# An FFT-mixing and gated-FFN kernel: fp32 first pass, filter scaling on VectorE in program order, and a second pass in two batch halves

## The chip, the cores and the metric

The kernel runs on one core of one Trainium2 chip. The metric is the device time of one execution in microseconds (us). A core has five engines with queues of their own: TensorE (PE in the profile) for matmuls, VectorE (DVE) and ScalarE (ACT) for elementwise work, GpSimd (POOL), and SyncE (SP), which here only starts transfers. Each engine takes its instructions in order. Transfers run on 16 DMA engines beside them. Matmuls write to PSUM, the other operands lie in SBUF, and inputs, outputs and large intermediates lie in HBM.

## The reference, cut to what matters

```python
# x: (8, 3008, 256) fp32, filt_r, filt_i: (1505, 256) fp32
X = np.fft.rfft(x, axis=1)                       # along the sequence
Y = X * (filt_r + 1j * filt_i)[None]
y = np.fft.irfft(Y, n=3008, axis=1)              # (8, 3008, 256)
t = y.reshape(24064, 256)
gate = np.maximum(t @ w_gate, 0)                 # w_gate, w_val: (256, 1536)
out  = (gate * (t @ w_val)) @ w_out              # w_out: (1536, 256)
```

## The kernel before

The length 3008 is split as 64 x 47, so that the transform becomes small matrix products. There are four stages:

- Tables: sine and cosine matrices are computed on the chip. GpSimd writes index grids, VectorE multiplies them and reduces them to one period, ScalarE takes the sine. The filters are loaded and scaled, and the weights of the FFN are loaded and cast to bf16.
- Pass A: a transform over 64 points (`W1blk`), from `x` to the HBM buffer `Abuf`.
- Pass B: for each of 33 frequencies `k1` a transform over 47 points (`F2m`), the product with the filter, and the inverse over 47 points (`I2t`, `I2u`), from `Abuf` to the HBM buffer `Dbuf`.
- Pass C: for each of 8 x 6 blocks of up to 512 tokens the inverse over 64 points (`M1`) and then the FFN, from `Dbuf` to the output.

All pools are given to a scheduler that places the instructions of each engine by its own estimate, so the order on an engine is not that of the source. The parts that matter, cut:

```python
# ---- tables: one grid is built for F2 (2 halves of k1) and for I2 (2 halves) ----
def center(dst, src, ncols, modulus): ...   # six VectorE operations on 128 x ncols
def build_vgrid(stage, ks, kn): ...         # two iotas, then 4 + 2 * 6 VectorE operations -> grs, grc
def put(mats, rofs, cofs, src, ks, kn, sgn): # ScalarE: sine of grs or grc into F2m, I2t or I2u
    ...
# ---- filters: one staging buffer fstg for four blocks (r and i, two halves of k1) ----
fstg = genf.tile([128, KH, D], FP32, tag="fstg")
fmir2 = genf.tile([128, KH, D], BF16, tag="fmir2")
for (src_hbm, dst_tile, imag) in ((filt_r, Ftr, False), (filt_i, Fti, True)):
    for (ks, kn) in ((0, 17), (17, 16)):
        for rofs in (0, 64):
            nc.gpsimd.dma_start(fstg[rofs:rofs + 24, :kn, :], ...)
            nc.scalar.activation(dst_tile[rofs:rofs + 24, ks:ks + kn, :],
                                 fstg[rofs:rofs + 24, :kn, :], AF.Copy, scale=1.0 / 3008.0)
        for r in range(23):                       # mirrored rows, one transfer each
            nc.gpsimd.dma_start(fstg[32 + r:33 + r, :kn, :], ...)
        nc.scalar.activation(fmir2[32:55, :kn, :], rev[32:55], AF.Copy, scale=sgn / 3008.0)
        for rofs in (0, 64):
            nc.gpsimd.dma_start(dst_tile[rofs + 24:rofs + 47, ks:ks + kn, :], fmir2[32:55, :kn, :])
# ---- FFN weights: GpSimd loads to stgw (one buffer per shape), ScalarE casts ----
...
# ---- pass A: 4 pairs of batches x 6 tiles ----
for q in range(B // 2):
    for c0 in range(0, N2, 8):
        asb = pa.tile([128, 8 * D], BF16, tag="asb", bufs=3)
        xf = pa.tile([128, 8 * D], FP32, tag="xf", bufs=2)
        ldeng.dma_start(xf[:, :cnt * D], ...)                  # 1 MB; SyncE and ScalarE by turns
        xb = pa.tile([128, 8 * D], BF16, tag="xb", bufs=2)
        nc.vector.tensor_copy(xb[:, :cnt * D], xf[:, :cnt * D])
        for cc0 in range(0, cnt, 2):
            ps = psA.tile([128, 2 * D], FP32, tag="psa", bufs=2)
            nc.tensor.matmul(ps[:, :w], W1blk, xb[:, cc0 * D:cc0 * D + w], start=True, stop=True)
            nc.scalar.copy(asb[:, cc0 * D:cc0 * D + w], ps[:, :w])
        for bl in range(2):                                    # two stores to Abuf
            steng.dma_start(Abuf[:, c0:c0 + cnt, 2 * q + bl, :], ...)
# ---- pass B: 33 frequencies, all 8 batches (2048 columns) in two parts c ----
for k1 in range(NK1):
    at = atiles[k1 % 4]                                        # [128, B * D]
    nc.sync.dma_start(at[0:48, :], Abuf[k1])                   # and a second half for 1 <= k1 <= 31
    for c in range(2):
        psX = psB.tile([128, 1024], FP32, tag="psx")           # 2 buffers
        ...                                                    # 2 matmuls F2m x at
        nc.vector.tensor_tensor(tt, psX3, _bcast_mid(Ftr[:, k1, :], 4), op=ALU.mult)
        nc.vector.tensor_tensor(uu, psX3, _bcast_mid(Fti[:, k1, :], 4), op=ALU.mult)
        psD = psB.tile([128, 1024], FP32, tag="psd")           # 2 buffers
        ...                                                    # 4 matmuls I2t x tt + I2u x uu
        nc.scalar.copy(dsb[:, cs], psD)
    steng.dma_start(Dbuf[k1], dsb[0:48, :])                    # and a second for 1 <= k1 <= 31
# ---- pass C: 48 blocks ----
for b in range(B):
    for (z0, nb) in n2_blocks:
        dblk = pcd.tile([64, 8, D], BF16, tag="dblk")          # 4 buffers
        nc.sync.dma_start(dblk[:, :nb, :], Dbuf[:, z0:z0 + nb, b, :])
        ...        # psY = M1 x dblk, yt; 12 x (psG, psV, vsb, prod); 4 x (psO over 12, osb, store)
```

Of the kernel before, what the change touches and what calls it, by code (L numbers as in the profile page):

```python
# [9 lines left out]
FP32 = mybir.dt.float32  # L10
BF16 = mybir.dt.bfloat16
I32 = mybir.dt.int32
AF = mybir.ActivationFunctionType
ALU = mybir.AluOpType
# [15 lines left out]
def kernel(  # L30
# [10 lines left out]
    nc = tc.nc  # L41
# [4 lines left out]
    NK1 = 33  # L46
    DFF = moe_w_gate.shape[1]
    NFT = DFF // 128
    assert S == N1 * N2 and D == 256 and DFF % 128 == 0

    consts = ctx.enter_context(tc.tile_pool(name="consts", bufs=1))
    dram = ctx.enter_context(tc.tile_pool(name="dram", bufs=1, space=bass.MemoryType.DRAM))

# [34 lines left out]
        nc.scalar.activation(out_ap, rem[sl], AF.Sin, bias=0.0,  # L88
                             scale=scale_sign * 2.0 * math.pi / modulus)

    W1blk = consts.tile([128, 128], BF16)
    nc.vector.memset(W1blk, 0.0)
    for blk in range(2):
        rs = blk * 64
# [29 lines left out]
    with tc.tile_pool(name="passA", bufs=4) as pa, \  # L124
# [80 lines left out]
        for (src_hbm, dst_tile, imag) in ((filt_r, Ftr, False), (filt_i, Fti, True)):  # L205
            for (ks, kn) in ((0, 17), (17, 16)):
                for rofs in (0, 64):
                    nc.gpsimd.dma_start(fstg[rofs:rofs + 24, :kn, :],
                                        _ap(src_hbm, ks * D, [[64 * D, 24], [D, kn], [1, D]]))
                    nc.scalar.activation(dst_tile[rofs:rofs + 24, ks:ks + kn, :],  # L210
                                         fstg[rofs:rofs + 24, :kn, :],
                                         AF.Copy, bias=0.0, scale=1.0 / 3008.0)
                for r in range(23):
                    k2 = 24 + r
                    first_row = 3008 - 64 * k2 - (ks + kn - 1)
                    nc.gpsimd.dma_start(fstg[32 + r:33 + r, :kn, :],
                                        _ap(src_hbm, first_row * D, [[1, 1], [D, kn], [1, D]]))
                rev = dataclasses.replace(
                    fstg, offset=fstg.offset + (kn - 1) * D,
                    ap=[list(fstg.ap[0]), [-D, kn], [1, D]])  # L220
                sgn = -1.0 if imag else 1.0
                nc.scalar.activation(fmir2[32:55, :kn, :], rev[32:55], AF.Copy,
                                     bias=0.0, scale=sgn / 3008.0)
                for rofs in (0, 64):
                    nc.gpsimd.dma_start(dst_tile[rofs + 24:rofs + 47, ks:ks + kn, :],
                                        fmir2[32:55, :kn, :])
# [8 lines left out]
                                              [[fdim_hbm, 128], [128 * fdim_hbm, kdim], [1, fstep]]))  # L235
                nc.scalar.copy(w_sb[:, :, ci * fstep:(ci + 1) * fstep], stgw)

        with tc.tile_pool(name="psA", bufs=1, space=bass.MemoryType.PSUM) as psA:
            for q in range(B // 2):
                for c0 in range(0, N2, 8):  # L240
                    cnt = min(8, N2 - c0)
                    asb = pa.tile([128, 8 * D], BF16, tag="asb", bufs=3)
                    xf = pa.tile([128, 8 * D], FP32, tag="xf", bufs=2)
                    ldeng = nc.sync if (c0 // 8) % 2 == 0 else nc.scalar
                    ldeng.dma_start(xf[:, :cnt * D],
                                    x_rs[q * 128:(q + 1) * 128, c0:c0 + cnt, :])
                    xb = pa.tile([128, 8 * D], BF16, tag="xb", bufs=2)
                    nc.vector.tensor_copy(xb[:, :cnt * D], xf[:, :cnt * D])  # L248
                    for cc0 in range(0, cnt, 2):
                        ccnt = min(2, cnt - cc0)  # L250
                        w = ccnt * D
                        ps = psA.tile([128, 2 * D], FP32, tag="psa", bufs=2)
                        nc.tensor.matmul(ps[:, :w], W1blk, xb[:, cc0 * D:cc0 * D + w],  # L253
                                         start=True, stop=True)
                        nc.scalar.copy(asb[:, cc0 * D:cc0 * D + w], ps[:, :w])  # L255
                    for bl in range(2):
# [3 lines left out]
                            Abuf[:, c0:c0 + cnt, b, :],  # L260
                            asb[bl * 64:(bl + 1) * 64, :cnt * D].rearrange("p (a d) -> p a d", d=D))


    with tc.tile_pool(name="passB", bufs=4) as pb, \
         tc.tile_pool(name="psB", bufs=2, space=bass.MemoryType.PSUM) as psB:
        na_bufs = 4
        atiles = []
        for i in range(na_bufs):
            t = pb.tile([128, B * D], BF16, tag="ak1", name=f"ak1_{i}", bufs=na_bufs)
            nc.vector.memset(t, 0.0)  # L270
            atiles.append(t)
        for k1 in range(NK1):
            at = atiles[k1 % na_bufs]
            dsb = pb.tile([128, B * D], BF16, tag="dsb", bufs=3)
            nc.sync.dma_start(at[0:48, :].rearrange("p (b d) -> p b d", d=D),
                              Abuf[k1, :, :, :])
            if 1 <= k1 <= 31:
                nc.sync.dma_start(at[64:112, :].rearrange("p (b d) -> p b d", d=D),
                                  Abuf[32 + k1, :, :, :])
            for c in range(2):  # L280
                cs = slice(c * 1024, (c + 1) * 1024)
                psX = psB.tile([128, 1024], FP32, tag="psx")
                for h in range(2):
                    hs = slice(c * 1024 + h * 512, c * 1024 + (h + 1) * 512)
                    nc.tensor.matmul(psX[:, h * 512:(h + 1) * 512], F2m[:, k1, :],  # L285
                                     at[:, hs], start=True, stop=True)
                tt = pb.tile([128, 4, D], BF16, tag="t", bufs=3)
                uu = pb.tile([128, 4, D], BF16, tag="u", bufs=3)
                psX3 = psX.rearrange("p (a d) -> p a d", d=D)
                nc.vector.tensor_tensor(tt, psX3, _bcast_mid(Ftr[:, k1, :], 4), op=ALU.mult)  # L290
                nc.vector.tensor_tensor(uu, psX3, _bcast_mid(Fti[:, k1, :], 4), op=ALU.mult)  # L291
                psD = psB.tile([128, 1024], FP32, tag="psd")
                for h in range(2):
                    os_ = slice(h * 512, (h + 1) * 512)
                    nc.tensor.matmul(psD[:, os_], I2t[:, k1, :],  # L295
                                     tt.rearrange("p a d -> p (a d)")[:, os_],
                                     start=True, stop=False)
                    nc.tensor.matmul(psD[:, os_], I2u[:, k1, :],  # L298
                                     uu.rearrange("p a d -> p (a d)")[:, os_],
                                     start=False, stop=True)  # L300
                nc.scalar.copy(dsb[:, cs], psD)  # L301
            steng = nc.scalar if (k1 % 2 == 0) else nc.sync
            steng.dma_start(Dbuf[k1, :, :, :],
                            dsb[0:48, :].rearrange("p (b d) -> p b d", d=D))
            if 1 <= k1 <= 31:
                steng.dma_start(Dbuf[32 + k1, :, :, :],
                                dsb[64:112, :].rearrange("p (b d) -> p b d", d=D))

    out_rs = out.rearrange("(b n1 n2) d -> b n1 n2 d", n1=N1, n2=N2)
    n2_blocks = [(z, min(8, N2 - z)) for z in range(0, N2, 8)]  # L310

# [83 lines left out]
```

## Time and profile before

| what | value |
|---|---|
| median of 5 runs | 1274.94 us (1274.26 to 1279.07) |
| profiled execution | 1274.26 us, span of the trace 1272.5 us |
| busy, share of the span | PE 77%, VectorE 60%, ScalarE 41%, GpSimd 6% |
| granted TensorE clock, mean | 0.989 |
| pass A, pass B | 24 casts of x on VectorE, 96 matmuls; 66 products `tt` and 66 `uu` |
| DMA | 111.51 MB, 88 GB/s over the span |

The profile is a page with the busy time of each engine, a strip of 40 slices, the chain of work that ended last, and groups of equal instructions; the trace behind it answers questions about stretches of time, about single instructions in order of time, and about waits. A line of the order of time gives the start, the length, the engine, the line of the source (L followed by a number), the operation, what is written from what, and in square brackets the idle time before it and what ended it. `ACTq`, `SPq` and `POOLq` are the parts of these engines that start transfers. An engine that is busy for a large share of the whole span may still be idle in the stage that decides, so stages are looked at one by one.

### The profile page before, as it was taken

The page shows a single profiled execution, that of the slowest core. Times are in us where ns is not written, and L with a number is a line of the kernel's source. Part 1 is how long each engine was busy: PE and PEld are TensorE (multiplying, and loading weights), DVE is VectorE, ACT ScalarE, POOL GpSimd, SP SyncE. Part 2 cuts the span into 40 slices and gives each one's busy share as a digit, 9 for nine tenths or more (in the row PEclk, how much of TensorE's full clock was granted, in tenths as well). Part 3 has the DMA queues.
Part 4 walks back from the last instruction along what each step waited for, and adds up shares of the span by engine and source line. Part 5 has one row for each costly group of instructions (what it writes and reads, how often), then busy time and mean ns, then how long its engine had stood idle before and what let it go on. Part 6 is the DMA issues. An engine that isn't in the chain of part 4 may idle for free.

```text
span 1272.5 us, 16253 instructions
## 1 busy us (share of the span) xinstructions
PE 984.8 (77%) x5852; PEld 512.4 (40%) x5852; DVE 765.6 (60%) x1151; ACT 517.7 (41%) x787; POOL 70.3 (6%) x139
## 2 busy tenths in 40 slices
PE   0324420465565999999999999999999999999998
PEld 0000000121121545555555545555555555555555
DVE  7971220698696665566655665566655665566655
ACT  3564443645543343334333343334333343334433
POOL 2130016400100000000000000000000000000000
PEclk9999999999798999999999999999999999999999
DMA  3779973665753111111111111111111111111111
GB/s 103 225 208 281 314 162 80 146 198 164 211 167 97 29 46 51 47 39 38 48 49 51 34 39 51 50 36 37 51 48 46 35 45 48 50 34 42 39 34 32
DMA packets 96257, 111.51 MB, mean 88 GB/s; under 512 B 11960, under 2 KB 85624, under 8 KB 93240
## 3 DMA queue, kind: packets, MB, share of 16 engines
q1 hardware_dynamic: 75280, 74.88, 20.8%
q10 hardware_dynamic: 16192, 24.51, 6.1%
q0 software_dynamic: 4704, 11.08, 3.7%
q8 instruction: 46, 0.75, 0.3%
q14 instruction: 35, 0.29, 0.1%
HBM read 59.06 MB, written 49.81 MB: 86 GB/s over the span
## 4 chain that ended last, share of the span: by engine, by line
PE 63%; DVE 4%; issue 1%; DMA 0%; ACT 0%; DVEq 0%
PE psG L337 22%; PE psO L354 20%; PE psV L340 20%; DVE yt L330 2%; DVE osb L358 2%; PE psY L326 1%; DMA Dbuf<-dsb 0%; DVE prod L345 0%; DVE uu L291 0%; ACT dsb L301 0%; PE psD L298 0%; ACT vsb L343 0%; PE psD L295 0%; DVEq L330 0%
## 5 line engine op out<-in xcount | busy, mean ns | idle before, releaser
L343 ACT CAST vsb<-psV 128x512 bf16<-128x512 f32 (+1 forms) x576 | 323.0, 578 | 539.7 <-PE psV L340 523.3
L345 DVE SCALAR_TENSOR_TENSOR prod<-psG,vsb 128x512 bf16<-128x512 f32 (+1 forms) x576 | 380.9, 679 | 196.5 <-ACT vsb L343 171.2
L337 PE MATMUL psG<-yt,WgT 128*128 128x512 bf16 (+1 forms) x1152 | 345.3, 374 | 34.8 <-DVE yt L330 33.9
L340 PE MATMUL psV<-yt,WvT 128*128 128x512 bf16 (+1 forms) x1152 | 354.9, 376 | 0.1
L354 PE MATMUL psO<-WoT,prod 128*128 128x256 bf16 (+1 forms) x2304 | 281.6, 273 | 0.0
L354 PEld LDWEIGHTS <-prod 128*128 128x128 bf16 (+1 forms) x2304 | 221.7, 98 | 57.4 <-DVE prod L345 10.7
L358 DVE COPY osb<-psO 128x256 f32<-128x256 f32 x192 | 81.5, 425 | 145.6 <-PE psO L354 145.6
L340 PEld LDWEIGHTS <-WvT 128*128 128x128 bf16 x1152 | 107.9, 97 | 148.6 <-issue 34.7
L337 PEld LDWEIGHTS <-WgT 128*128 128x128 bf16 x1152 | 111.7, 97 | 138.1 <-issue 38.5
L253 PE MATMUL ps<-xb,W1blk 128*128 128x512 bf16 x96 | 51.0, 587 | 121.2 <-DVE xb L248 80.2
L298 PE MATMUL psD<-uu,I2u 128*128 128x512 bf16 x132 | 51.8, 396 | 98.6 <-DVE uu L291 98.6
L291 DVE TENSOR_TENSOR uu<-psX,Fti 128x1024 bf16<-128x1024 f32 x66 | 80.1, 1216 | 54.6 <-DMA Fti<-fmir 54.6
L301 ACT CAST dsb<-psD 128x1024 bf16<-128x1024 f32 x66 | 66.5, 1012 | 73.0 <-PE psD L298 68.3
L290 DVE TENSOR_TENSOR tt<-psX,Ftr 128x1024 bf16<-128x1024 f32 x66 | 80.2, 1217 | 12.7 <-PE psX L285 9.1
L253 PEld LDWEIGHTS <-W1blk 128*128 128x128 bf16 x96 | 9.7, 113 | 161.7 <-issue 71.3
L255 ACT CAST asb<-ps 128x512 bf16<-128x512 f32 x96 | 52.2, 579 | 50.7 <-PE ps L253 49.4
L295 PEld LDWEIGHTS <-I2t 128*128 128x128 bf16 x132 | 12.9, 98 | 147.7 <-issue 120.2
L248 DVE CAST xb<-xf 128x2048 bf16<-128x2048 f32 (+1 forms) x24 | 28.7, 1202 | 66.7 <-DMA xf<-in_x_dram 60.6
L330 DVE CAST yt<-psY 128x512 bf16<-128x512 f32 (+1 forms) x96 | 60.3, 669 | 9.1 <-PE psY L326 9.1
L295 PE MATMUL psD<-tt,I2t 128*128 128x512 bf16 x132 | 52.6, 398 | 10.3 <-ACT dsb L301 5.5
L326 PEld LDWEIGHTS <-dblk 64*128 64x128 bf16 x752 | 30.2, 95 | 57.0 <-issue 56.1
L326 PE MATMUL psY<-M,dblk 64*128 64x64 bf16 x752 | 46.5, 193 | 7.6 <-issue 7.6
(74 smaller groups left out, 288.2 us busy)
## 6 DMA issues: line engine op xcount, KB each, us to landing
out_dram<-osb SPq DMA_DIRECT2D x376, 64.0 KB, 2.0
xf<-in_x_dram SPq DMA_DIRECT2D x12, 1024.0 KB, 7.2
ak<-Abuf SPq DMA_DIRECT2D x64, 192.0 KB, 3.5
dblk<-Dbuf SPq DMA_DIRECT2D x40, 256.0 KB, 3.4
xf<-in_x_dram ACTq DMA_DIRECT2D x8, 1024.0 KB, 6.9
Dbuf<-dsb ACTq DMA_DIRECT2D x32, 192.0 KB, 3.6
Dbuf<-dsb SPq DMA_DIRECT2D x32, 192.0 KB, 3.2
Abuf<-asb SPq DMA_DIRECT2D x20, 256.0 KB, 4.6
```

The lines of the kernel that those rows point to most:

```text
L290: nc.vector.tensor_tensor(tt, psX3, _bcast_mid(Ftr[:, k1, :], 4), op=ALU.mult)
L291: nc.vector.tensor_tensor(uu, psX3, _bcast_mid(Fti[:, k1, :], 4), op=ALU.mult)
L295: nc.tensor.matmul(psD[:, os_], I2t[:, k1, :], tt.rearrange("p a d -> p (a d)")[:, os_], start=True, stop=False)
L301: nc.scalar.copy(dsb[:, cs], psD)
L326: nc.tensor.matmul(psY[:, j * 64:(j + 1) * 64], dblk[:, j, h * 128:(h + 1) * 128], M1, start=(j == 0), stop=(j == nb - 1))
L330: nc.vector.tensor_copy(yt[:, :ntok], psY[:, :ntok])
L337: nc.tensor.matmul(psG[:, :ntok], WgT[:, h, ft * 128:(ft + 1) * 128], yts[h][:, :ntok], start=(h == 0), stop=(h == 1))
L340: nc.tensor.matmul(psV[:, :ntok], WvT[:, h, ft * 128:(ft + 1) * 128], yts[h][:, :ntok], start=(h == 0), stop=(h == 1))
L343: nc.scalar.copy(vsb[:, :ntok], psV[:, :ntok])
L345: nc.vector.scalar_tensor_tensor(prod[:, :ntok], in0=psG[:, :ntok], scalar=0.0, in1=vsb[:, :ntok], op0=ALU.max, op1=ALU.mult)
L354: nc.tensor.matmul(psO[:tw, :D], prods[ft][:, t_i * 128:t_i * 128 + tw], WoT[:, ft, :], start=(ft == 0), stop=(ft == NFT - 1))
L358: nc.vector.tensor_copy(osb[:tw], psO[:tw, :D])
```

## The change

The change takes VectorE out of pass A and gives it the filters, and it lets pass C's first reads depend on half of pass B only:

1. `tc.manual_schedule` for VectorE: from the start to the end of pass B, VectorE runs its instructions in the order of the source, not in the scheduler's. The other engines are placed by the scheduler as before.
2. Pass A multiplies in fp32: `W1blk` is an fp32 table, the matmul reads `xf` directly, the cast to `xb` is gone, and `xf` has three buffers in place of two.
3. The filters are scaled on VectorE in place of ScalarE.
4. Pass B goes over the 33 frequencies twice, each time for four of the eight batches. The tiles `ak` and `dsb` and their transfers have half the size,[...] and the pools of pass A and pass B are open at the same time.

```diff
+    region = ctx.enter_context(ExitStack())
+    region.enter_context(tc.manual_schedule(engines={mybir.EngineType.DVE}))
...
-    W1blk = consts.tile([128, 128], BF16)
+    W1blk = consts.tile([128, 128], FP32)
...
-                    nc.scalar.activation(dst_tile[rofs:rofs + 24, ks:ks + kn, :],
-                                         fstg[rofs:rofs + 24, :kn, :],
-                                         AF.Copy, bias=0.0, scale=1.0 / 3008.0)
+                    nc.vector.tensor_scalar(dst_tile[rofs:rofs + 24, ks:ks + kn, :],
+                                            fstg[rofs:rofs + 24, :kn, :],
+                                            scalar1=1.0 / 3008.0, scalar2=None, op0=ALU.mult)
...
-                nc.scalar.activation(fmir2[32:55, :kn, :], rev[32:55], AF.Copy,
-                                     bias=0.0, scale=sgn / 3008.0)
+                nc.vector.tensor_scalar(fmir2[32:55, :kn, :], rev[32:55],
+                                        scalar1=sgn / 3008.0, scalar2=None, op0=ALU.mult)
...
-                    xf = pa.tile([128, 8 * D], FP32, tag="xf", bufs=2)
+                    xf = pa.tile([128, 8 * D], FP32, tag="xf", bufs=3)
...
-                    xb = pa.tile([128, 8 * D], BF16, tag="xb", bufs=2)
-                    nc.vector.tensor_copy(xb[:, :cnt * D], xf[:, :cnt * D])
...
-                        nc.tensor.matmul(ps[:, :w], W1blk, xb[:, cc0 * D:cc0 * D + w],
+                        nc.tensor.matmul(ps[:, :w], W1blk, xf[:, cc0 * D:cc0 * D + w],
                                          start=True, stop=True)
...
-        for k1 in range(NK1):                        # all 8 batches
-            at = atiles[k1 % na_bufs]                # [128, B * D], 4 buffers
+            def pass_b_half(half):
+                b0 = half * 4
+                for k1 in range(NK1):                # batches b0 .. b0 + 3
+                    at = atiles[ait % na_bufs]       # [128, 4 * D], 4 buffers
+                    nc.sync.dma_start(at[0:48, :], Abuf[k1, :, b0:b0 + 4, :])
...                                                   # psX of 1024 columns, tt and uu as before
+                    for c in range(2):
+                        psD = psB.tile([128, 512], FP32, tag="psd", bufs=2)
...                                                   # I2t x tt, I2u x uu
+                        nc.scalar.copy(dsb[:, cs], psD)
+                    steng.dma_start(Dbuf[k1, :, b0:b0 + 4, :], dsb[0:48, :])
...
+            for q in range(4):
+                pass_a_pair(q)
+            pass_b_half(0)
+            pass_b_half(1)
+
+    region.close()
```

(Cut: the rearrangements of the access patterns, the second transfers for `1 <= k1 <= 31`, and the unchanged lines.)

## The prediction

> **What bounds the kernel now.** I read first the chain that ended last, then the busy time by stage, then the order of time on ScalarE and VectorE around the stage borders.
>
> The chain on the page, by engine:
>
> ```profile
> PE 63%; DVE 4%; issue 1%; DMA 0%; ACT 0%; DVEq 0%
> ```
>
> It names only TensorE, and it runs almost entirely through the last stage, which the diff does not touch. So the question is when that stage starts. The busy time in five stretches (start:end, length, busy us per engine, clock, DMA share, GB/s):
>
> ```profile
> 0.00:87.00 87.00, 14.88 (x28) 3.07 (x29) 74.00 (x135) 41.96 (x56) 25.77 (x51) 1.00 0.57 174
> 87.00:173.00 86.00, 36.17 (x69) 6.67 (x67) 19.05 (x16) 40.93 (x74) 0.00 (x0) 1.00 0.86 271
> 188.00:236.00 48.00, 2.02 (x5) 0.69 (x5) 2.36 (x2) 22.82 (x7) 26.54 (x56) 1.00 0.39 86
> 236.00:402.00 166.00, 102.54 (x386) 33.30 (x384) 145.36 (x128) 81.58 (x74) 13.13 (x23) 0.95 0.60 174
> 407.00:1272.00 865.00, 826.00 (x5360) 467.64 (x5357) 518.81 (x864) 322.97 (x576) 0.00 (x0) 1.00 0.16 43
> ```
>
> Each stretch has its own limit: VectorE (74 of 87 us) while tables are built and pass A starts; DMA (86%) for the rest of pass A; nothing at all from 188 to 236; VectorE (145 of 166) in pass B; TensorE (826 of 865) in pass C. The hole from 188 to 236 shows in the order of time on ScalarE (start, length, instruction, wait before it):
>
> ```profile
> 172.88 0.61 ACTq L259 DMA_DIRECT2D Abuf<-asb  x1
> 173.82 3.83 ACT L222 ACTIVATE fmir<-fstg 23x4352 bf16<-23x4352 f32 x1 [0.97 <-ACT asb L255]
> ...
> 201.57 3.62 ACT L222 ACTIVATE fmir<-fstg 23x4096 bf16<-23x4096 f32 x1 [9.51 <-DMA fstg<-in_filt_i_dram]
> ...
> 223.42 3.83 ACT L222 ACTIVATE fmir<-fstg 23x4352 bf16<-23x4352 f32 x1 [6.73 <-DMA fstg<-in_filt_i_dram]
> ```
>
> The first filter block was loaded by about 89 us, but its scaling sits in ScalarE's queue behind the last pass-A copy. One buffer `fstg` serves four blocks, so the chain load, scale, reload starts at 174 and takes 22 to 27 us a block. VectorE pays for it:
>
> ```profile
> 232.71 2.36 DVE L291 TENSOR_TENSOR uu<-psX,Fti 128x1024 bf16<-128x1024 f32 x2 [45.69 <-DMA Fti<-fmir]
> ```
>
> At the border to pass C, TensorE waits for the last store and reload of Dbuf:
>
> ```profile
> 398.85 0.38 PE L298 MATMUL psD<-uu,I2u 128*128 128x512 bf16 x1
> ...
> 406.83 0.37 PE L326 MATMUL psY<-M,dblk 64*128 64x64 bf16 x4 [7.60 <-issue]
> ```
>
> [...] No run here shows an fp32 matmul yet; it is the largest unmeasured cost. [...] pass-A matmuls start 0.43 us apart, those of pass B 0.22 us, though the granted clock is 1.00 in both. [...] In the trace 12 filter loads took 7.32 us on GpSimd (0.61 each) beside busy VectorE and 0.48 beside an idle one: small.
>
> **The change part by part.**
>
> *1. Casts leave VectorE.* 24 casts of about 1.2 us (28.7 us in the groups) go; eight of them lie before 87 us. VectorE now runs in program order: small tables (about 52 dependent operations at 0.2 us and the start, near 13 us, and 2.5 of wait for M1f behind the first matmuls), three memsets of 1.82, then four grids. One grid without casts takes 11.2 us in the trace (75.8 to 87.0). So 15.5 + 5.5 + 4 x 11.4 + about 3 of waits = 70 us, against 87: minus 17. By then, as now at 87, about 8 of 24 x-tiles are through, because ScalarE's sine writes sit between the copies and wait for the grids.
>
> *2. fp32 matmuls in pass A.* [...] A tile has four: 4 us. The DMA now needs 5.1 us a tile (16 casts from 87.3 to 168.9), so TensorE fits under it[...]. The third xf buffer makes up for holding xf through the matmuls.
>
> *3. Filter scaling moves to VectorE.* 24x4352 took 3.83 us on ScalarE; the VectorE cast of 128x2048 took 1.22 us from SBUF, so about 2.4 us. Of more weight is its place: it comes after the grids and two memsets of 3.58 and so starts at 70 + 7 = 77 us, under pass A. First block done at about 84. A later block took 22 us (205.5 to 227.5); faster scaling takes off 1.5, but loads in a full DMA take longer: GpSimd waits for the load eight earlier, and 23 row loads at a latency of 5 instead of 3 us add about 5. So 26 a block: 84 + 3 x 26 = 162 us. Pass B's first product comes after that in VectorE's order.
>
> *4. Pass A ends.* Remaining work from 72 us is what took from 87 to 173 before: 86 us. In it now lie three filter blocks, at 31% of the DMA for 48 us over two blocks, or 7.5 us each: plus 22. Three buffers and an earlier start should raise the DMA share from 86% towards 95%: minus 10. 72 + 86 + 22 - 10 = 170. From the last copy to the first product took 12 us (172.8 to 184.7: store, load, matmul, and a little filter wait); I take 10. Pass B starts at 180, and the filter chain (162) is hidden with 18 to spare. Before, it ran from 232.7: 53 us gained.
>
> *5. Pass B in two halves of four batches.* As many products as before, of the same shape: 2 x 66, one each 1.133 us in steady state (239.86, 241.00, 242.13): 149.5 us. It took 165.7 (232.7 to 398.4); the late last filter block (8.9) and stalls for psX (9.1) made most of the rest. The filter waits go; the weight casts stay in ScalarE's queue ahead of some dsb copies, single-buffered: I leave 8 us. DMAs double in number at half the size: 4 in 2.27 us, landing in about 3.5; four `ak` buffers give 9 us of lead, enough. ScalarE copies two of 0.59 instead of one of 1.01 per 1024 columns: no bound. 180 + 149.5 + 8 = 337.5.
>
> *6. Border and pass C.* The first `dblk` tiles need only the first half of Dbuf, stored long before, so they are prefetched; the 7.6 us wait falls away and psY follows the last matmul, at about 339. Built, the changed program has pass C's instructions in the same order on every compute engine, but for the first two blocks on TensorE. Before, it took 1272.5 - 406.8 = 865.7. End 1204.5; the median before lies 2.4 above the profiled span: about 1206.
>
> Sum of the gains: 53 at the hole, 8 in pass B, 7.5 at the border: 68.5 us.
>
> **Rivals.**
> - *TensorE bounds pass A.* [...]2 us a matmul, 8 a tile, 16 tiles: pass A ends at 72 + 130 = 202, total near 1238. For it: no row shows such a matmul[...].
> - *The filter chain takes the place of pass A as the bound.* With latencies of 8 us, 34 us a block: 186, total near 1212. For it: the 86% DMA share. VectorE's strict order makes any lateness count in full.
> - *Pass A hides nothing:* what the filters took alone they take from the x loads; the plus 22 is that. If the share does not rise, 180 instead of 170: 1216.
> - *Stalls in pass B:* smaller DMAs and weight casts cost 20 instead of 8: 1218. If grids and DMA go better than thought, pass A ends at 155: 1190.
>
> **Range and chances.** Pass A's end carries plus or minus 12, pass B's stalls plus or minus 8, and the lean is upward[...]. Predicted 1206 us, 1188 to 1228 eight times in ten. Faster by over 2% means under 1249.4; even the worst rival stays below it, and only two rivals together would pass it: 0.93 faster, 0.05 within 2%, 0.02 slower.
>
> **What would show it.** The fp32 matmul's mean near 1 us and TensorE under 80% busy in pass A; `fmir` scaling on VectorE from about 82 us and its fourth at about 160; the first steady `tt` at 180, preceded by a wait for psX or the ak load and not for a filter; tt and uu back to back for 150 us; psY within 2 us of the last pass-B matmul; pass C 865 us long. A wait for `fstg` in front of the fourth `fmir` later than 175, or matmuls of 1.7 us and more, would prove steps 3 or 2 wrong.

## The result, and the profile after

| | before | after |
|---|---|---|
| median | 1276.47 us (16 runs, 1272.38 to 1280.44) | 1217.09 us (9 runs, 1213.77 to 1227.27) |
| ratio after / before | | 0.9547, 95% interval 0.9522 to 0.9573 |
| profiled span | 1272.5 us | 1214.8 us |
| pass C's first matmul | 406.83 us | 352.11 us |

The kernel is 4.5% faster. Pass C takes 862.7 us (1214.8 - 352.1) against 865.7, so nearly the whole gain is the time at which pass C starts. The chain that ended last, by engine, on the page of the changed kernel:

```profile
PE 66%; DVE 4%; issue 0%; ACT 0%; DVEq 0%
```

DMA has left the chain (the last Dbuf store and reload were in it before). The busy time in six stretches of the changed kernel (start:end, length, then busy us and count for PE, PE weight load, VectorE, ScalarE, GpSimd, then clock, DMA share, GB/s):

```profile
0.00:75.00 75.00, 40.68 (x67) 14.90 (x68) 63.66 (x125) 38.07 (x61) 24.93 (x50) 0.84 0.69 218
75.00:163.00 88.00, 67.19 (x126) 23.66 (x124) 30.66 (x11) 37.72 (x66) 35.19 (x55) 0.85 0.96 284
163.00:189.00 26.00, 0.00 (x0) 0.00 (x0) 9.25 (x5) 0.41 (x2) 17.61 (x29) 0.56 0.42 108
189.00:197.00 8.00, 1.01 (x2) 0.14 (x2) 1.99 (x5) 2.94 (x2) 2.66 (x4) 0.50 1.04 228
197.00:351.00 154.00, 118.14 (x394) 33.83 (x394) 149.36 (x132) 75.29 (x135) 1.55 (x3) 0.97 0.65 185
352.00:1214.00 862.00, 823.52 (x5360) 466.93 (x5359) 518.92 (x864) 323.06 (x577) 0.00 (x0) 1.00 0.16 43
```

The hole of 48 us (188 to 236 before) has not gone: it has shrunk to 34 us, from 163 to 197. In its first 26 us TensorE does nothing and the DMA is busy for 42%. What fills it is seen in VectorE's order of time (start, length, instruction, in brackets the wait before it and what ended it):

```profile
73.30 0.94 DVE L154 TENSOR_TENSOR grc<-grc,gq 128x752 f32<-128x752 f32 x1
...
87.81 4.68 DVE L224 TENSOR_SCALAR fmir<-fstg 23x4352 bf16<-23x4352 f32 x1
...
127.72 2.28 DVE L224 TENSOR_SCALAR fmir<-fstg 23x4096 bf16<-23x4096 f32 x1 [18.08 <-DMA fstg<-in_filt_r_dram]
...
160.54 4.67 DVE L224 TENSOR_SCALAR fmir<-fstg 23x4352 bf16<-23x4352 f32 x1 [13.92 <-DMA fstg<-in_filt_i_dram]
...
186.36 2.28 DVE L224 TENSOR_SCALAR fmir<-fstg 23x4096 bf16<-23x4096 f32 x1 [9.34 <-DMA fstg<-in_filt_i_dram]
188.81 2.11 DVE L270 MEMSET ak<- 128x512 uint32 x4 [0.17 <-issue]
196.76 1.22 DVE L294 TENSOR_TENSOR tt<-psX,Ftr 128x1024 bf16<-128x1024 f32 x1 [5.84 <-PE psX L289]
```

The four blocks of the filter end at 92.5, 130.0, 165.2 and 188.6: 37.5 and 35.2 us apart while pass A's transfers run, 23.4 once they are over. From the second on, each waits for a load into `fstg`. Pass B's first product stands behind the fourth. The memsets of `ak` stand there too, so the loads of `ak` cannot be asked for earlier; SyncE's waits (line, what it waited for, us in total, times, longest) have it, although the half of `Abuf` that is read had been complete for long (shown below):

```profile
SPq L281 <- DVE ak L270: 25.2, 1, 25.2
```

TensorE at both ends of pass B, in the order of time:

```profile
161.38 1.56 PE L256 MATMUL ps<-xf,W1blk 128*128 128x512 f32 x4 [0.23 <-ACT asb L258]
195.71 1.01 PE L289 MATMUL psX<-ak,F2m 128*128 128x512 bf16 x2 [32.77 <-DMA ak<-Abuf]
...
350.58 0.59 PE L302 MATMUL psD<-uu,I2u 128*128 128x512 bf16 x2 [0.35 <-DVE uu L295]
352.11 0.62 PE L336 MATMUL psY<-M,dblk 64*128 64x64 bf16 x16 [0.94 <-ACT dsb L305]
```

At the border to pass C the wait of 7.60 us is now 0.94. The fp32 matmuls have their own group on the page:

```profile
L256 PE MATMUL ps<-xf,W1blk 128*128 128x512 f32 x192 | 107.9, 712 | 55.1 <-ACT asb L258 38.5
```

There were 96 instructions and the group has 192 records: an fp32 matmul leaves two. In TensorE's order of time (the last line comes after a pause):

```profile
82.17 3.79 PE L256 MATMUL ps<-xf,W1blk 128*128 128x512 f32 x8 [0.23 <-ACT asb L258]
86.17 3.79 PE L256 MATMUL ps<-xf,W1blk 128*128 128x512 f32 x8 [0.22 <-ACT asb L258]
...
147.04 3.78 PE L256 MATMUL ps<-xf,W1blk 128*128 128x512 f32 x4 [4.09 <-ACT asb L258]
```

Eight records take 3.79 us in the first two lines, where most start 0.43 us apart and the granted clock is 1.00 (79 to 97 us). Four take 3.78 us in the last, where they start 0.85 us apart and the clock is 0.50 (147 to 151 us). The mean of 0.85 in pass A is made of such stretches.

### The profile page after: what moved, and what is told of

It reads as the page before. It is cut to its first block, busy times and chain, and to the rows that moved or that the text cites. A ratio compares the mean times of both kernels' runs of the same rounds, so it can differ in the third digit from the quotient of the medians.

```text
span 1214.8 us, 16712 instructions
## 1 busy us (share of the span) xinstructions
PE 1050.7 (86%) x5948; PEld 539.5 (44%) x5948; DVE 773.8 (64%) x1139; ACT 478.5 (39%) x841; POOL 81.9 (7%) x139
## 4 chain that ended last, share of the span: by engine, by line
PE 66%; DVE 4%; issue 0%; ACT 0%; DVEq 0%
PE psG L347 23%; PE psO L364 21%; PE psV L350 21%; DVE yt L340 2%; DVE osb L368 2%; PE psY L336 2%; DVE uu L295 0%; ACT dsb L305 0%; ACT vsb L353 0%; PE psD L302 0%; DVEq L340 0%
## 5 line engine op out<-in xcount | busy, mean ns | idle before, releaser
L256 PE MATMUL ps<-xf,W1blk 128*128 128x512 f32 x192 | 107.9, 712 | 55.1 <-ACT asb L258 38.5
L305 ACT CAST dsb<-psD 128x512 bf16<-128x512 f32 x132 | 71.1, 589 | 74.9 <-PE psD L302 73.4
L256 PEld LDWEIGHTS ps<-xf,W1blk 128*128 128x128 f32 x192 | 38.6, 225 | 124.0 <-ACT asb L258 93.7
L289 PE MATMUL psX<-ak,F2m 128*128 128x512 bf16 x132 | 40.9, 389 | 36.7 <-DMA ak<-Abuf 34.6
L302 PE MATMUL psD<-uu,I2u 128*128 128x512 bf16 x132 | 41.5, 388 | 19.0 <-DVE uu L295 15.4
L224 DVE TENSOR_SCALAR fmir<-fstg 23x4352 bf16<-23x4352 f32 (+1 forms) x4 | 13.9, 3479 | 41.4 <-DMA fstg<-in_filt_i_dram 23.3
```

What stands on the lines that cost most here:

```text
L256: nc.tensor.matmul(ps[:, :w], W1blk, xf[:, cc0 * D:cc0 * D + w], start=True, stop=True)
```

## The experiments

Runs are best compared by their ratios: the kernel before, run beside each, had medians from 1273.6 to 1278.9 us. Differences in us below are of medians or of traces; the ratios put some of them up to 6 us higher or lower, so no single part is known more finely than that. "Free" is where pass B's products start to run on with both filters; psY is pass C's first matmul. Runs marked * use only the upper 16 bits of each word of x in pass A.

| run | us | ratio to before (95%) | last pass-A matmul ends | last fmir ends | free | psY |
|---|---|---|---|---|---|---|
| changed kernel | 1217.1 | 0.9547 (0.9522-0.9573) | 162.9 | 188.6 | 196.8 | 352.1 |
| e1_memset_early | 1216.6 | 0.9508 (0.9494-0.9522) | 184.5 | 191.5 | 191.6 | 350.1 |
| e2_rows_ahead | 1205.8 | 0.9430 (0.9415-0.9445) | 175.8 | 174.6 | 182.0 | 341.8 |
| e4_filters_act | 1239.3 | 0.9677 (0.9648-0.9705) | 171.8 | (ScalarE) | 206.6 | 374.4 |
| e5_bf16_high * | 1212.3 | 0.9479 (0.9460-0.9497) | 145.2 | 182.1 | 190.1 | 345.2 |
| e6_interleaved | 1224.3 | 0.9600 (0.9574-0.9626) | 171.0 | 191.3 | 199.4 | 359.2 |
| e7_manual_only | 1299.1 | 1.0198 (1.0178-1.0218) | 217.0 | (ScalarE) | 256.4 | 432.7 |
| e8_all * | 1195.9 | 0.9388 (0.9369-0.9406) | 158.5 | 175.0 | 175.1 | 331.5 |
| e9_rows_first * | 1197.6 | 0.9396 (0.9368-0.9425) | 150.0 | 170.6 | 170.7 | 332.9 |
| e10_no_rows | 1206.5 | 0.9444 (0.9419-0.9469) | 206.1 | 149.1 | 166.1 | 342.3 |
| e11_rows_first2 * | 1197.5 | 0.9364 (0.9313-0.9416) | 158.6 | 178.6 | 178.6 | 336.7 |
| e12_no_manual | 1210.7 | 0.9478 (0.9454-0.9501) | 176.4 | 224.8 | 178.2 | 346.2 |
| e13_half_filters * | 1203.5 | 0.9446 (0.9415-0.9477) | 161.3 | 213.3 | 164.8 | 336.7 |

My theory after reading the trace: the filter chain, stretched by a full DMA, sets pass B's start, with the `ak` memsets behind it. Rivals: pass A's own end sets it; the fp32 matmuls set it.

### The ak memsets ahead of the filters

```diff
+        # pool akp opened with the table pools, memsets before the filter loop
+        for i in range(na_bufs):
+            t = akp.tile([128, 4 * D], BF16, tag="ak1", name=f"ak1_{i}", bufs=na_bufs)
+            nc.vector.memset(t, 0.0)
...
-                t = pb.tile([128, 4 * D], BF16, tag="ak1", name=f"ak1_{i}", bufs=na_bufs)
-                nc.vector.memset(t, 0.0)
```

> The changed kernel with one thing moved: the four ak memsets stand ahead of the filter scaling in VectorE's order. Theory (pass B's start is set by the filter chain, and then by the ak loads that wait for memsets queued behind it): the loads from Abuf start soon after pass A's end at 163 us, and the first tt follows the fourth fmir scaling (188.6 us) at once, at about 189 in place of 196.8. About 8 us less: 1209 us. Rival (the loads are bound by the last stores to Abuf or by the DMA): the first tt stays near 196, 1217 us.

First SyncE's order of time in this run, then VectorE's:

```profile
109.94 0.81 SPq L282 DMA_DIRECT2D ak<-Abuf  x2
```

```profile
189.26 2.28 DVE L231 TENSOR_SCALAR fmir<-fstg 23x4096 bf16<-23x4096 f32 x1 [11.71 <-DMA fstg<-in_filt_i_dram]
191.57 1.23 DVE L295 TENSOR_TENSOR tt<-psX,Ftr 128x1024 bf16<-128x1024 f32 x1
```

The first product follows the last scaling without a gap, so the 8 us between them are gone. Its psX had been written from 115.16 us on; VectorE took it in its turn, behind the fourth block. But the chain itself ends 3 us later and pass A 22 us later, so the start gains 5 us, and stalls for psX early in pass B (7.2 us in place of 4.2) give 3 of them back: psY moves by 2 us. The expected time (1209) was missed: the median fell by only 0.5 us; the ratio fell by 0.0039, which is 5 us, and the two intervals meet at 0.9522. The run shows something more useful: the loads of `ak` went out at 110 us, while pass A ran until 184. Pass B's first half reads batches 0 to 3 only, the first two of pass A's four pairs. Pass A's end is no condition of pass B's start.

### The mirrored rows a block ahead

```diff
-                for r in range(23):                      # rows of this block, after its 24-row loads
-                    nc.gpsimd.dma_start(fstg[32 + r:33 + r, :kn, :], ...)
+            mb = 32 + 64 * (n % 2)                       # two places for rows, partitions 32 and 96
+            if n + 1 < len(blocks):
+                load_rows(n + 1)                         # the next block's 23 rows, ahead of this fmir
```

> The changed kernel with a second staging region for the mirrored rows (partitions 96 to 118 of the same buffers), and the row loads of a filter block issued before the scaling of the block ahead of it. No work is taken away. Theory (the chain of 23 row loads, scaling and store per block, 35 to 38 us each beside pass A's DMA, is what pass B waits for): the fourth fmir scaling falls from 186 to about 150 us, pass A's end (163) becomes the bound, the first tt comes at about 175: 1217 - 21 = 1196 us. Rival (the DMA as a whole is full, and the rows cost pass A what the chain gains): pass A ends at 175 or later and the first tt stays above 187: 1208 us or more.

Busy time of this run in one stretch, columns as above:

```profile
75.00:165.00 90.00, 66.56 (x122) 22.61 (x120) 32.88 (x11) 36.04 (x64) 50.41 (x76) 0.87 1.00 289
```

The DMA is busy for all of it (1.00, against 0.95 in the changed kernel), the chain ends 14 us earlier (expected: 150), and pass A 13 us later (expected: unchanged). The theory is half right: the rows do wait for one another behind `fstg`, and issuing them ahead takes 11 us off the time (15 by the ratios); but they then take DMA time from pass A. How the two press on each other shows in the changed kernel: a row of 17 KB lands in 3.0 us (median) before 75 us, at a DMA share of 0.69, and in 5.5 us from 75 to 163 us, at 0.96.

### bf16 instead of fp32 in pass A

```diff
-    W1blk = consts.tile([128, 128], FP32)
+    W1blk = consts.tile([128, 128], BF16)
...
-    nc.tensor.matmul(ps[:, :w], W1blk, xf[:, a:a + w], ...)
+    xhi = xf.bitcast(BF16).rearrange("p (n two) -> p n two", two=2)
+    nc.tensor.matmul(ps[:, :w], W1blk, xhi[:, a:a + w, 1], ...)   # upper 16 bits of each word
```

> The changed kernel with pass A's matmul in bf16 again, without a cast: W1blk is bf16 and the moving operand is the upper half of each fp32 word of xf, read with a step of two, so x is cut to bf16 and not rounded. [...] Theory (fp32 matmuls lie under the DMA and pass B's start is set by the filter chain): matmul time in pass A falls by more than half, but the first tt stays at 190 to 198 us: 1210 to 1219 us. Rival[...]: pass A ends 15 us or more earlier, the row loads get free DMA sooner and the time falls to 1205 us or less.

Busy time of this run in the same stretch:

```profile
75.00:165.00 90.00, 26.18 (x49) 4.81 (x48) 35.41 (x13) 31.47 (x56) 41.58 (x64) 1.00 0.85 247
```

TensorE is busy for 26 us in place of 67, and pass A ends 18 us earlier, but pass B starts only 6.7 us earlier, because the chain does (182.1 against 188.6). Time and start fell where the theory put them: fp32 costs 5 to 9 us (median, traces, ratios), by way of the chain, and it is not the bound. The rival, by which the fp32 matmuls slow the tiles and with them the DMA, had its early end of pass A, but not its time (1205 or less).

### No mirrored rows at all

The 92 row loads are taken out and those rows of `fstg` zeroed once, so this run leaves out the upper half of the filter. The weights of the FFN, no longer behind the rows in GpSimd's queue, are asked for at 17 to 47 us in place of 184 to 213.

```diff
-                for r in range(23):
-                    nc.gpsimd.dma_start(fstg[32 + r:33 + r, :kn, :], ...)
+        nc.gpsimd.memset(fstg[32:64], 0.0)               # once
```

> The changed kernel without the 92 transfers of mirrored filter rows: those rows of fstg are zeroed once, and everything else (24-row loads, scalings, stores of fmir) stays, so the upper half of the filter is left out. GpSimd's queue being free, the FFN weights are loaded among the grids. Theory (the mirrored rows are what makes the filter chain long, and by sharing the DMA they also hold pass A): pass A ends at 146 to 156, the chain ends before it, and the first product comes at 155 to 166: 1176 to 1190 us. Rival (the chain is long by its other transfers, the 24-row loads and the stores of fmir that land in 8 to 11 us each in a full DMA, one after the other through one buffer): last fmir scaling at 165 or later, first product at 173 or later, 1195 us or more.

The order of time on VectorE, and then on SyncE, in this run:

```profile
146.81 2.28 DVE L220 TENSOR_SCALAR fmir<-fstg 23x4096 bf16<-23x4096 f32 x1 [3.67 <-DMA Fti<-fmir]
...
166.13 1.22 DVE L290 TENSOR_TENSOR tt<-psX,Ftr 128x1024 bf16<-128x1024 f32 x1 [14.77 <-PE psX L285]
...
186.69 1.22 DVE L290 TENSOR_TENSOR tt<-psX,Ftr 128x1024 bf16<-128x1024 f32 x1 [11.54 <-PE psX L285]
```

```profile
152.75 1.88 SPq L277 DMA_DIRECT2D ak<-Abuf  x2
...
161.75 0.58 SPq L258 DMA_DIRECT2D Abuf<-asb  x1
164.02 0.35 SPq L246 DMA_DIRECT2D xf<-in_x_dram  x1
170.53 0.59 SPq L258 DMA_DIRECT2D Abuf<-asb  x1
171.21 0.57 SPq L277 DMA_DIRECT2D ak<-Abuf  x1
```

Without rows the chain ends at 149, so the rows make 40 us of it. The time did not follow: of 31 us by which the first product comes earlier only 10 reach psY. Pass B now runs beside the last part of pass A, whose end moved to 206. Its `ak` loads stand in SyncE's queue between loads and stores of pass A, and those asked for by 165 us take 11.3 us (median) to land. Pass B takes 175 us instead of 154. The theory's chain and start held; its end of pass A (146 to 156) and its time did not; the rival's time held and its chain did not. A new wait, which neither had named, took the gain back.

### Undoing one part

The scaling back on ScalarE:

```diff
-    nc.vector.tensor_scalar(dst, fstg..., scalar1=1.0 / 3008.0, ...)     # both places
+    nc.scalar.activation(dst, fstg..., AF.Copy, bias=0.0, scale=1.0 / 3008.0)
```

> The changed kernel with the filter scaling put back on ScalarE; all else as changed. Theory (what counts is when the chain runs, not the engine): ScalarE's queue holds the first fmir scaling behind 20 of 24 tiles of pass A, about 145 us, blocks two and three take 22 to 27 us each, the first uu comes at about 205 and the fourth block stalls pass B later as it did before the change: 1228 to 1238 us. Rival one (moving the scaling is nearly all of the gain): 1250 us or more. Rival two (it gives nothing, the chain is DMA-bound anyway): 1217 us.

VectorE's order of time in this run:

```profile
161.44 1.22 DVE L294 TENSOR_TENSOR tt<-psX,Ftr 128x1024 bf16<-128x1024 f32 x1 [76.28 <-DMA Ftr<-fmir]
206.55 1.23 DVE L295 TENSOR_TENSOR uu<-psX,Fti 128x1024 bf16<-128x1024 f32 x1 [43.89 <-DMA Fti<-fmir]
...
258.50 1.23 DVE L295 TENSOR_TENSOR uu<-psX,Fti 128x1024 bf16<-128x1024 f32 x1 [9.84 <-DMA Fti<-fmir]
```

The old hole is back (43.9 us for `Fti`, 45.7 before the change): moving the scaling is worth 22 us by the medians (1239 against 1217) and 17 by the ratios. The time came out just above the expected range.

Pass B over both halves at each frequency:

```diff
-            for k1 in range(NK1):                                        # called for each half
+            for k1, b0 in [(k, b) for k in range(NK1) for b in (0, 4)]:  # called once
```

> The changed kernel with the tiles of half size, but pass B goes through both halves of the batches at each frequency, so that the first half of Dbuf is complete only 2.3 us before the second. Theory (the two loops of pass B are worth only the wait at the border, because pass C's first reads are prefetched): pass B starts at 197 and lasts 154 as in the changed kernel, and psY waits 4 to 8 us after the last matmul of pass B, as the 7.60 before the change: 1221 to 1225 us. Rival 1 (the halved tiles themselves make pass B shorter or the border shorter): the time stays at 1217. Rival 2 (the late wait comes back and the order of the two loops also stalls pass B, because the four ak buffers are used up faster): over 1228.

TensorE's order of time at the border to pass C in this run:

```profile
354.00 0.59 PE L301 MATMUL psD<-uu,I2u 128*128 128x512 bf16 x2 [0.35 <-DVE uu L294]
359.16 1.03 PE L334 MATMUL psY<-M,dblk 64*128 64x64 bf16 x16 [4.57 <-DMA dblk<-Dbuf]
```

The wait for `dblk` is back, at 4.57 us, and pass B lasts 154.6 us as before. The two loops are worth 7 us at the border and at the start (free at 199.4 against 196.8), and nothing inside pass B, as the theory said. The intervals of the two ratios just fail to overlap.

Source order on VectorE alone, in the kernel before:

```diff
+    region.enter_context(tc.manual_schedule(engines={mybir.EngineType.DVE}))   # to the end of pass B
```

> The kernel before, with VectorE in source order to the end of pass B and nothing else. Theory (source order only pays because the casts of x are gone from VectorE): all casts stand after the grids and the two memsets of 3.58, so pass A's first matmul comes at about 83 us instead of 33 and pass A ends at 200 to 206 instead of 173; the last filter blocks stay behind it on ScalarE; pass B's products run freely from 240 to 255 instead of 233: 1280 to 1300 us, slower than before. Rival (the order of VectorE alone gives the gain, fp32 is not needed): 1217 to 1230 us, pass B from about 200.

The first cast of `x` comes at 80.80 us, behind the grids, and the first matmul at 82.01; pass A ends at 217, later than expected, and the time, 2.0% above the kernel before, lies in the expected range. Source order is harmful as long as the casts stand in it.

The change without source order:

```diff
-    region.enter_context(tc.manual_schedule(engines={mybir.EngineType.DVE}))
```

> The changed kernel without the source order on VectorE: the scheduler orders it, with fp32 pass A, the filters on VectorE and the halves of pass B kept. In its order the first two products of pass B stand ahead of the scalings of the second to fourth filter block. Theory (source order is what keeps the filter chain ahead of pass B in VectorE's queue): pass A ends at 148 to 160, the first two products come at 158 to 168, the other blocks only after them at some 23 us each, so that the products run freely from 220 to 240: 1235 to 1255 us. Rival (with the casts gone the order is of no account): 1210 to 1220 us.

VectorE's order of time in this run:

```profile
118.63 1.23 DVE L293 TENSOR_TENSOR tt<-psX,Ftr 128x1024 bf16<-128x1024 f32 x1 [22.97 <-PE psX L288]
124.52 1.22 DVE L293 TENSOR_TENSOR tt<-psX,Ftr 128x1024 bf16<-128x1024 f32 x1 [4.66 <-PE psX L288]
...
178.18 2.36 DVE L294 TENSOR_TENSOR uu<-psX,Fti 128x1024 bf16<-128x1024 f32 x2 [6.08 <-DMA Fti<-fmir]
...
222.47 2.28 DVE L223 TENSOR_SCALAR fmir<-fstg 23x4096 bf16<-23x4096 f32 x1
230.06 2.36 DVE L294 TENSOR_TENSOR uu<-psX,Fti 128x1024 bf16<-128x1024 f32 x2 [5.30 <-DMA Fti<-fmir]
```

My theory was wrong by 24 us or more: I had the two early products wait for pass A's end. They came at 118.6 and 124.5, with pass A running to 176, and so held nothing up. The scheduler lets the products of k1 below 17 run from 178, when three blocks are there, and scales the fourth inside pass B. That is better than source order: 0.9478 against 0.9547, intervals apart. Source order on VectorE is no part of the gain; it costs 6 us by the medians and 9 by the ratios. The rival's time (1210 to 1220) was met.

### Versions meant to be faster

Rows ahead, early memsets and upper bf16 halves together (the three diffs above):

> Rows loaded a block ahead, the ak memsets ahead of the filter scaling, and pass A on the upper bf16 halves of x (W1blk in bf16; x is cut to its upper 16 bits in pass A) together. Theory (with the matmuls short the transfers decide: the DMA is full from 75 us, and the chain of filter blocks ends only where its transfers get through): pass A ends at 150 to 155, the last fmir scaling at 160 to 168, the first product directly after it at 165 to 172: 1188 to 1198 us. Rival (the transfers of pass A and of the filters only change places, and the end of the two together stays where it was with rows ahead alone): first product at 180, 1203 to 1208 us.

VectorE at the end of the chain in this run:

```profile
172.75 2.29 DVE L241 TENSOR_SCALAR fmir<-fstg 23x4096 bf16<-23x4096 f32 x1
175.07 1.23 DVE L306 TENSOR_TENSOR tt<-psX,Ftr 128x1024 bf16<-128x1024 f32 x1
```

1195.9 us, in the expected range, though its marks came 3 to 7 us late. It is the fastest of the versions together with the next two. The DMA share is 0.91 from 12 to 40 us, 0.81 to 75 and 0.97 to 165.

The same, with the rows of the first two blocks asked for among the grids:

```diff
+            load_rows(0 if ks == 0 else 1)       # after each of the two I2 grids, in source order
...
+            if n + 2 < len(blocks):
+                load_rows(n + 2)                 # after block n's fmir and its stores
```

> As the run before (rows ahead, early ak memsets, upper bf16 halves), but the mirrored rows of the first two filter blocks are asked for among the grids, from about 12 to 75 us, where the DMA of the changed kernel was busy for 0.56 to 0.77 of the time, and the FFN weights after the filters. Theory (what sets pass B's start is when the rows go through a full DMA after 75 us): two of the four blocks are scaled by 95, the last fmir scaling comes at 130 to 140, pass A ends at 140 to 145, the first product at 148 to 155: 1168 to 1180 us. Rival (ScalarE's queue decides: the sines of the last grid stand behind pass A's last copy there, and GpSimd's index writes wait behind the rows): the grids end 20 us later or more, first product at 165 or later: 1188 us or more.

GpSimd's order of time in this run (issues of transfers, with the waits before them):

```profile
145.55 1.91 POOL L196 DMA_DIRECT2D fstg<-in_filt_i_dram  x4 [0.80 <-DMA fstg<-in_filt_i_dram]
147.45 1.00 POOL L230 DMA_DIRECT2D fstg<-in_filt_i_dram  x2
```

Two blocks were scaled by 108 (the theory said 95), but the third only at 163: its 24-row loads stand behind all 46 rows of the last two blocks. The rival's time held, but not its reason: the grids end at 75 as before, and the sines that stand behind pass A's last copy (151 to 158) hold nothing up. To ask whether GpSimd's order alone did this, the fourth block's rows were put behind the third block's 24-row loads:

```diff
-            if n + 2 < len(blocks):
-                load_rows(n + 2)                 # after block n's fmir and its stores
+            if 1 <= n < len(blocks) - 1:
+                load_rows(n + 1)                 # before block n's fmir
```

> As the run with the rows of the first two blocks among the grids, but the rows of the fourth block are asked for after the third block's 24-row loads instead of ahead of them. Theory (in that run GpSimd's queue held the third block, whose rows were there by 130 and which was scaled at 158; the DMA had room): third fmir scaling at 128 to 136, fourth at 148 to 156, pass A ends at 148 to 152, and the sines of the last grid, which stand behind pass A's last copy, let the first product come at 155 to 163: 1178 to 1188 us. Rival (the DMA's total of x, Abuf and filters sets the end of both, whatever the order of GpSimd): the first product stays at 167 to 175, 1190 to 1198 us.

The third block's 24-row loads on GpSimd in this run:

```profile
131.66 0.99 POOL L230 DMA_DIRECT2D fstg<-in_filt_i_dram  x2
```

Issued 16 us earlier, these loads still landed late: their scalings began at 143.7 and 149.3, and the last block's scaling ended at 178.6, later than in the run before. The theory fell; the rival's time held, and its mark (first product at 167 to 175) was missed by 3.6 us. The trace is of the longest of this version's four runs (1202.3 us; the shortest took 1186.6). The three versions cannot be told apart by their intervals: with a full DMA the order only moves the wait.

At last, two filter blocks before pass B and two inside it:

```diff
-                  for (src, dst, imag) in (r, i) for (ks, kn) in ((0, 17), (17, 16))]
+                  for (ks, kn) in ((0, 17), (17, 16)) for (src, dst, imag) in (r, i)]
...
+                    if half == 0 and k1 in (8, 15):
+                        filter_block(2 if k1 == 8 else 3)
```

> As the run with rows ahead, early ak memsets and upper bf16 halves together, but the filter blocks come in the order real and imaginary for k1 below 17, then real and imaginary for the rest, and VectorE scales the third and the fourth block inside the first half of pass B, at its k1 = 8 and k1 = 15; the FFN weights are asked for after them. Theory (pass B's first half needs two filter blocks and the first two of four batch pairs only; after that, ScalarE's queue, where the copies of pass B stand behind the last copy of pass A, is the next to decide): second fmir scaling at 112 to 120, the first product directly after it, the products run freely from pass A's end at 150 to 160, pass C's first matmul at 316 to 328: 1180 to 1192 us. Rival 1 (all four blocks are needed before pass B runs, or the transfers of pass B and of the last blocks only push each other): pass C's first matmul at 331 or later, 1195 us or more. Rival 2 (the first half of pass B runs beside the second half of pass A without being held by ScalarE): pass C's first matmul before 305, under 1170 us.

VectorE where pass B begins in this run:

```profile
121.11 1.22 DVE L315 TENSOR_TENSOR tt<-psX,Ftr 128x1024 bf16<-128x1024 f32 x1
139.82 1.23 DVE L316 TENSOR_TENSOR uu<-psX,Fti 128x1024 bf16<-128x1024 f32 x1 [17.49 <-DMA Fti<-fmir]
...
164.84 1.22 DVE L315 TENSOR_TENSOR tt<-psX,Ftr 128x1024 bf16<-128x1024 f32 x1 [21.53 <-PE psX L310]
```

The start is as the theory said: the first product directly after the second block, and the third pair at 164.8, once ScalarE had done pass A's last copy (at 161.8) and copied the first two of pass B. Then two filter blocks and their waits lie inside pass B, which takes 172 us from there, and the time is 1203: the theory's sum missed by 11 us and rival 1's time held. All versions with the bf16 halves have psY between 331 and 345 us, whatever stands where.

## Why the prediction was right or wrong

The time was predicted well (1206, measured 1217, range 1188 to 1228), and the steps less well:

1. Casts leave VectorE: right but for 4 us. The grids end at 74.2 instead of 70.
2. fp32 matmul of 1.0 us, pass A not bound by TensorE: right. The 1.0 was the author's estimate, as no run had shown an fp32 matmul, and it is not the bare cost. From 82.17 us four matmuls take 3.79 us and the next four follow after 4.0. Two records 0.43 us apart make 0.86 us a matmul, which is four times the 0.216 us from one bf16 matmul to the next in the kernel before (from 413 us on), and the rest is mostly waits for ScalarE's copies out of `ps`. Matmuls of 1.7 us, a sign against this step, appeared as well (two records 0.85 us apart, as from 147.04 us, where two matmuls take 3.78 us, near the rival's 2 us each), but TensorE was busy for only 67.19 of the 88 us from 75 to 163, or 76%, and e5_bf16_high shows that fp32 was not the bound.
3. **The step that failed.** "So 26 a block: 84 + 3 x 26 = 162 us" became 188.6. Of the 26.6 us missed, 8.5 lie in the first block (the late grids 4.2, gaps at the memsets 1.8, and 2.5 of scaling, most of it a reversed one of 4.68 us where 2.4 was assumed) and 18.1 in the next three (37.5, 35.2 and 23.4 instead of 26 each). The term that was too small is what a full DMA adds to a block: 5 us, for rows that land in 5 us instead of 3. The 17 KB rows did land in 5.5 us. But the block's other transfers slowed down too (below), and GpSimd waits for them in the same queue. In the third block the second 24-row load was asked for at 133.03 us and its scaling began at 144.20, 11.2 us later; before the change the same load took 6.4 us (206.46 to 212.86). The rows behind it waited on GpSimd until stores of the second block's `fmir` had landed (GpSimd's and VectorE's order of time):

```profile
133.03 0.50 POOL L210 DMA_DIRECT2D fstg<-in_filt_i_dram  x1
...
139.59 0.49 POOL L218 DMA_DIRECT2D fstg<-in_filt_i_dram  x1 [3.66 <-DMA Ftr<-fmir]
142.08 0.48 POOL L218 DMA_DIRECT2D fstg<-in_filt_i_dram  x1 [2.01 <-DMA Ftr<-fmir]
144.20 2.42 DVE L212 TENSOR_SCALAR Fti<-fstg 24x4352 bf16<-24x4352 f32 x1 [11.75 <-DMA fstg<-in_filt_i_dram]
```

Each of these two waits is for the transfer that GpSimd had issued eight before. Even without any rows (e10_no_rows) the last three blocks took 51.2 us, 17 each. The prediction's own sign came: the wait for `fstg` ahead of the fourth `fmir` ended at 186.36, later than 175. The rival with the filter chain as the bound was the right one, and the prediction had it. That its 186 lies so near 188.6 is partly luck: it reckoned 34 us a block from 84, with landings of 8 us, and the blocks took 32 on average from 92.5.
4. "The filter chain (162) is hidden with 18 to spare" failed with it, and its frame was wrong too: pass B's start was reckoned from pass A's end (163 measured, 170 predicted). e1_memset_early and e12_no_manual show that pass A's end is not the condition. What the prediction lacked is the queue: the `ak` memsets and the first product both stand behind the fourth block on VectorE. Chain 188.6, then memsets, load and matmul 8.1: 196.8 instead of 180. The sign named for a hidden chain, a first `tt` that waits for psX and not for a filter, was met all the same (5.84 us), because the load behind psX stood behind the chain.
5. Pass B: 153.8 us (196.76 to 350.53) instead of 157.5. The products' 149.5 were right; stalls were 4.2, not 8.
6. Border and pass C: right, psY 1.6 us after the last product, and pass C 3.0 us shorter. Before, TensorE came into it after the wait of 7.60 us: the granted clock is 0.50 from 403 to 413 us, with matmuls 0.43 us apart from 408.6 to 412.0, and 0.22 apart at 1.00 from 413 on. After the change it is 1.00 from 352 us on, with 0.22 from 353.3. Part of the 3.0 us lies there; whether the missing pause is the reason was not tried.

So 16.8 us too late at the start, of which 3.8 and 3.0 came back: some 10 over the 1204.5 us of span. That the time fell in the range is owed to the range, which left 22 us upward, and to these two returns; the term it rests on most, the chain's end, was 26.6 us off. What the parts are worth, by undoing them (medians, then ratios): the filters on VectorE 22 or 17 us, the two loops of pass B 7, source order minus 6 or minus 9. The other 36 to 43 of some 58 us are left to the casts that are gone and the third buffer of `xf`; neither was undone by itself, so this share is not shown, and parts that meet in one queue need not add up.

That the full DMA is the next bound, up to 165 us, is read from its shares and from three reorderings of e8_all that gave nothing (e9_rows_first, e11_rows_first2, e13_half_filters). A kernel that moves fewer bytes there was not tried, except e10, whose gain went into pass B's stalls.

## What to carry to other kernels

When work moves to another engine's queue, ask what stands behind it there: here the chain of filter blocks took pass A's place as the bound, and a memset that needs nothing kept loads waiting for 25 us (moving it alone gained little, because the chain still stood ahead of the first product). A chain load, scale, reload through one buffer should be timed with the landing times of a full DMA and not with those of an idle one; here the block grew from 23 to 36 us. Splitting a pass by batches does more than help its successor: the first part no longer needs all of its predecessor, and that is worth using only when queues and transfers let both run side by side.

## What the runs showed of the hardware

- In the changed kernel a scaling on VectorE with a reversed read of 17 rows of 256 (23x4352) took 4.68 us, with 16 rows (23x4096) 2.28, while 17 rows read forward (24x4352) took 2.42. Why the reversed 17 rows took so long was not shown; the runs have no other numbers of rows.
- The changed kernel's mean granted clock of 0.85 from 75 to 165 us is made of 1.00 and 0.50 by turns: 1.00 from 79 to 97 us, with the records of fp32 matmuls 0.43 us apart, and 0.50 from 147 to 151, after a pause of 4.09 us, with records 0.85 apart. So fp32 matmuls ran at both; what sets the turns was not shown.
- A clock shown as 1.00 does not always go with the same distance between starts. In the kernel before it is 1.00 from 413 to 420 us, with bf16 matmuls 0.22 us apart, and 1.00 in pass A too (87 to 173 us), with bf16 matmuls 0.40 us apart at 148.70 and 0.49 at 150.45; the prediction gave 0.43 for pass A beside the 1.00. The clock records in this trace begin only at 239.0 us, so the 1.00 ahead of them may be no reading at all. The distance between starts is the surer sign.
- In the full DMA of the changed kernel (share 0.96 from 75 to 163 us) 17 KB rows landed in 5.5 us against 3.0 before it (share 0.69 up to 75 us), 195 KB stores of `fmir` in 9.6, against 4.5 from 163 to 200 us, and 408 KB loads in 10.2, against 6.2 up to 75 us (medians).
